# A hybrid convolution and MLP block on one core: diagonals made by GpSimd selects, larger buffer rings and another hand-written order

## The chip, the core and the metric

The kernel runs on one core of a Trainium2 chip. A core has a matrix engine (TensorE, in the profile PE, with its weight loads PEld), a vector engine (VectorE, DVE), an activation engine (ScalarE, ACT), a general engine (GpSimd, POOL) and a sequencer for transfers (SyncE, SP; SPq is its queue). The engines run side by side and wait for one another through semaphores. Operands lie in an on-chip memory of 128 partitions, matmuls write to eight PSUM banks of 128 x 512 f32, and transfers run on 16 DMA engines. The metric is the device time of one execution in microseconds (us), lower is better.

## What is computed

S = 2048 rows, D = 512 channels, F = 1792; inputs and output are bf16.

```python
def _A_ref(q, k, v, shift_k, ssm_k, ssm_D):      # ks = 4
    for t in range(ks):
        k_shift = k_shift + k_pad[:, t:t + S, :] * shift_k[:, ks - 1 - t][None, None, :]
    kv = k_shift * v
    y = irfft(rfft(pad(kv)) * rfft(pad(ssm_k)))[:S]
    y = y + kv * ssm_D
    return q * y
def _B_ref(x, w1, w2, w3, w4):
    h = gelu(layernorm(x) @ w1)
    hs = concat(four quarters of h, shifted by +1, -1, +2, -2 rows) @ w2
    x1 = x + hs
    return x1 + gelu(layernorm(x1) @ w3) @ w4
h = A_q + _A_ref(layernorm(A_q), A_k, A_v, A_shift_k, A_ssm_k, A_ssm_D)
return h + _B_ref(layernorm(h), B_w1, B_w2, B_w3, B_w4)
```

So a four-tap filter over the rows of k, a gate by v, a long convolution over the rows with one filter for each channel, a gate by q, and then a block of two small matmuls with row shifts and an MLP from 512 to 1792 to 512 channels.

## The kernel before, in words

The rows are cut into two halves, s = 0 and 1, of eight blocks of 128 rows. The long convolution is done by matmuls: a two-step transform of the filter (signals F0 and F1) and of the gated k (A0 and A1), products of the spectra, and a two-step inverse. Everything is cut into 812 named tasks. `plan.add` (from L268 on) lists them with their engines and dependencies, and the string `ORDER` (L31 on) fixes by hand which task comes next, on which engine (S for SP, P for PE, V for DVE, A for ACT, G for POOL, M for a double-width eviction on ACT) and in which buffers. Each engine runs its own tasks in the order of that string, and waits at a task until its inputs are there; nothing behind it on that engine passes it. The DMA queue is SP's: the loads, the transfers between the transform's steps and the stores all go through it in order.

In what follows a task is called by its name and indices:

- Lk, Lf, Lv, Lq: loads of k (transposed, with the taps in the last columns of each row), the convolution filter, v and q; the first index is the half.
- skf.c (L298): copies the four taps of channel block c, bf16, from the loaded k to f32 scalars `sskf`. dg.c (L300 to L312): from them four 128 x 128 diagonal matrices in `diag`, each the identity times one tap, by four instructions on DVE (L309) or ACT (L307).
- K.gc (L444): the four-tap filter as seven matmuls against the diagonals, for half a half (g = 0 to 3) and channel block c. KV.gc (L452): the gate by v, on DVE, out of PSUM.
- S1 (L391), E1, X (L407), S2 (L415), E2: first transform step, its eviction out of PSUM (L259, on ACT or DVE), the transfer that turns the partitions, the second step, and its eviction. For F1 the second eviction adds F0's spectrum (L427, DVE).
- P (L476): products of the spectra, 128 x 1024, all on DVE, into a ring `prs` of four buffers. I2 (L486): the inverse's first step, EV its eviction into a ring `vst` of two, XI (L497) its transfer, I1 (L504) its second step. There are 16 products for s = 0 and 32 for s = 1.
- bits, cons, ftv, fta, ft, ttv, tta, tts, f2v, f2a, f2s, tt, f2: building the transform's tables in several steps that go to and fro between DVE, POOL and ACT. `cons` (L331 to L335, POOL) needs `bits` (L324 to L328, DVE); ft is the table that S2 needs.
- dr (L296): adds ssm_D to the filter's first row. Q, QV, QP, QN: statistics of q. Y (L616): normalised q, into a ring `z_t` of two. H (L619): the gate, with the residual. HS, uw, rr, hn, hb: the layer norm of H.
- LT, TE (L673, L259): transposes by PE and their evictions; for some pairs of blocks they are two writes to memory and a transposing load on SP instead (L666, L668). xT holds the transposed blocks, a ring of three. W (L702) and U (L706): the first matmul and its gelu. X2 (L725), S, SS, R: the second matmul with the row shifts, and its sums. ux, r1, xn, lb, LX, EX: the second layer norm and transposes. M (L780), G (L784), O (L793), Z (L795), OUT: the MLP's two matmuls, the gelu, the last sum and the store.

Each half has its W, X2, M and O tasks. The MLP of s = 0 runs among the products of s = 1.

Of the kernel before, what the change touches and what calls it, by code (L numbers as in the profile page):

```python
# [17 lines left out]
KW = NB * 129 + 4  # L18
# [13 lines left out]
002S 004S 003S 005S 031V 041V 042G 043G 000S 029P0 030P 059P23 001S 007S 061P45 006S 062V 067P67 010S 033V 037V 032V 069P01 008S 070V 009S 060A 068A  # L32
034V 063P23 064A 065P45 066A 023S 049G 022S 038A 035V 091P60 039V 055P23 099P71 100V 036A 044V 056A 057P45 058A 040V 101P0 102V 103P1 104V 050V 045A
355V 051A 046G 047V 105P7 106V 048A 093P2 095P3 076S 119P45 120A 094V 115P01 354V 077S 054G 024S 075S 015S 096V 097P7 078S 116A 074S 073S 092V 098V
020S 071S 358V 121P23 122A 117P45 107P01 357V 053G 108A 118V 072S 111P67 113P23 021S 114V 016S 127S 109P01 112A 110A 123S 088P4567 089V 128S 090A
085P0123 087A 082P4567 083A 356V 086V 231P21 084A 079P4501 232V 124S 080V 081A 129S 125S 131P6723 130S 134P0145 132V 133A 136A 126S 144V0 143V1 352V
147V2 146V3 135A 014S 137P2367 019S 233P4 011S 139A 018S 145P01670 154V0 153V1 138A 148P 157V2 149A 156V3 223P50 224V 150A 155P01231 158P 159M 160A
187P67 353V 344S 229P5 234V 163V0 164V1 017S 151S 152S 230V 012S 351V 188A 140P0123 141A 235P4 142A 166V2 167V3 161S 162S 165P67010 168P 173V0 013S
359G 169A 174V1 227P5 170A 171S 172S 176V2 175P23671 177V3 178P 180A 199P01 228V 237P5 179V 236V 200A 181S 182S 238V 225P6 226V 343S 360G 361G 052A
362V0 191P23 193P01 192A 189P45 190A 194V 204S 203S 195P67 196A 201P23 202V 197P01 198A 183P45 239P67 365G1 366V 371G1 367A 207S 241P23 208S 184P01  # L40
363V 368G0 364A 242V 243P45 245P23 240A 369V 386G 372V 244A 246A 210S 373A 374V0 209S 206S 205S 257S 387G 185P67 247P01 377V1 375V 380G0 248A 378V
214P2345 215V 370A 249P67 250A 379A 388G 399V 186P01 381V 027S 255S 389G0 392G1 251P23 252A 253P67 254A 376A 383G1 390P00 393P2 259S 216V 211P4567
394V 391A 395P3 258S 384V 212V 382A 220P0145 400G 401G 402A2 405A3 403P21 404A 346S 213V 412G 413G 221V 406P6 397P7 347V 396A 263P0123 385A 398A 407V
# [802 lines left out]
```

## Time and profile before

| what | us |
|---|---|
| three runs: median, lowest, highest | 217.25, 216.3, 217.52 |
| the profiled execution, its device time | 216.0 |
| its span (first to last instruction in the trace) | 214.2 |
| PE busy in it | 198.7 |
| DVE, ACT, POOL busy | 147.9, 128.3, 72.3 |

The span is what the trace shows; 1.8 us of the device time lie outside it. A row of the list of groups gives the line, the engine, the operation, what it writes and reads, the count, then the busy time, the mean of one in ns, and the idle time of the engine just before with what ended it. A row of the timeline gives the start, the duration, the engine, the line and, in brackets, the idle time before it. A row of the table by stretches gives the length of the stretch and the busy time of each engine in it.

### The profile page before, as it was taken

Reading aid. Unit: us, or ns where it says so; the run is one execution under the profiler, and the core shown is the slowest. Engines: PE = TensorE matmul, PEld = TensorE weight load, DVE = VectorE, ACT = ScalarE, POOL = GpSimd, SP = SyncE. Lnnn points to the kernel's source line nnn. Section 1 sums busy time; section 2 is a strip of 40 time slices with the busy share of each in tenths; the row PEclk is TensorE's granted clock in tenths of the full one; section 3 lists DMA queues with packets and bytes.
Section 4 is the critical chain, followed back from the end, with each engine's and each line's share of the span. In section 5 each row is a group of like instructions: output and inputs, shape, how many; then the busy total and the mean of one; then the engine's idle time right before and its main releaser. Section 6 shows DMA issues by size and latency. Waiting matters only on the chain.

```text
span 214.2 us, 5136 instructions
## 1 busy us (share of the span) xinstructions
PE 198.7 (93%) x1980; PEld 114.8 (54%) x1980; DVE 147.9 (69%) x331; ACT 128.3 (60%) x210; POOL 72.3 (34%) x194
## 2 busy tenths in 40 slices
PE   7699858898979999999999999799999999999993
PEld 5254324342246646644655774466788887444441
DVE  7999998998999999889894985318687000005621
ACT  4678987889999676961960896345445757000000
POOL 7943000593786436400005883304615000000000
PEclk9999999999999999999999999999999999999998
DMA  6999699978679965030553015850644400000212
GB/s 197 343 386 340 251 362 329 231 203 296 244 252 300 408 249 150 0 100 1 77 148 101 2 23 113 163 122 13 160 99 104 117 2 0 3 0 24 97 50 73
DMA packets 30809, 32.85 MB, mean 153 GB/s; under 512 B 20545, under 2 KB 22594, under 8 KB 30530
## 3 DMA queue, kind: packets, MB, share of 16 engines
q1 hardware_dynamic: 30786, 32.54, 50.0%
q8 instruction: 15, 0.25, 0.5%
q14 instruction: 8, 0.07, 0.1%
HBM read 13.13 MB, written 4.46 MB: 82 GB/s over the span
## 4 chain that ended last, share of the span: by engine, by line
PE 73%; ACT 9%; DMA 7%; issue 4%; DVE 3%; SPq 3%; DVEq 0%; ACTq 0%
PE ps L780 23%; PE ps L793 21%; PE ps L725 6%; PE ps L702 6%; PE ps L486 6%; ACT r_a L259 3%; PE ps L444 3%; DMA r_dg<-dhb 2%; PE ps L504 2%; DMA r_fx<-in_fx_dram 2%; PE ps L415 2%; ACT r_z L259 2%; PE ps L391 2%; ACT junk L603 2%; DMA r_z<-r_vs 2%
## 5 line engine op out<-in xcount | busy, mean ns | idle before, releaser
L780 PEld LDWEIGHTS <-r_k 128*128 128x128 bf16 x448 | 43.2, 98 | 9.4 <-issue 3.2
L795 DVE TENSOR_TENSOR r_v<-ps,r_v 128x512 bf16<-128x512 f32 x16 | 10.7, 687 | 39.4 <-issue 31.4
L780 PE MATMUL ps<-r_dg,r_k 128*128 128x256 bf16 x280 | 32.9, 273 | 0.0
L476 DVE TENSOR_TENSOR r_p<-r_a,r_f 128x1024 bf16<-128x1024 bf16 x48 | 30.7, 685 | 2.5 <-PE ps L486 1.9
L259 ACT CAST r_a<-ps 128x1024 bf16<-128x1024 f32 x25 | 24.2, 1021 | 1.2 <-PE ps L391 0.6
L780 PE MATMUL ps<-xtx,r_k 128*128 128x256 bf16 x168 | 20.2, 273 | 0.0
L728 DVE SCALAR_TENSOR_TENSOR r_q<-r_v,hrr,ps 128x512 bf16<-128x512 bf16 x16 | 11.8, 741 | 9.0 <-PE ps L725 8.9
L444 PE MATMUL ps<-r_dg,r_k 128*128 128x256 bf16 (+3 forms) x112 | 16.0, 288 | 2.1 <-ACT r_f L259 1.7
L486 PE MATMUL ps<-r_p,ttab 32*64 32x512 bf16 x384 | 15.6, 383 | 1.2 <-DVE r_p L476 0.5
L259 ACT CAST r_vs<-ps 128x1024 bf16<-128x1024 f32 (+1 forms) x14 | 14.5, 1075 | 3.2 <-PE ps L486 2.3
L444 PEld LDWEIGHTS <-r_k 128*128 128x128 bf16 x112 | 9.3, 98 | 11.0 <-issue 5.6
L702 PEld LDWEIGHTS <-r_fx 128*128 128x128 bf16 x128 | 12.2, 98 | 5.4 <-issue 1.5
L751 POOL TENSOR_TENSOR xrr<-xrr,mhalf 128x2 f32<-128x2 f32 x8 | 7.0, 876 | 20.4 <-DVE xrr L748 20.0
L784 ACT ACTIVATE r_v<-ps 128x512 bf16<-128x512 f32 x14 | 8.0, 596 | 9.7 <-PE ps L780 9.6
L702 PE MATMUL ps<-r_dg,r_fx 128*128 128x256 bf16 x96 | 11.8, 273 | 1.7 <-DMA r_dg<-dhb 1.2
L603 ACT ACTIVATE junk<-r_v 128x512 bf16<-128x512 bf16 x14 | 9.0, 642 | 6.8 <-DVE r_v L619 5.9
L793 PE MATMUL ps<-w4s,r_kv 128*128 128x512 bf16 x56 | 12.7, 379 | 0.0
L619 DVE SCALAR_TENSOR_TENSOR r_v<-ps,qsd,z_t 128x512 bf16<-128x512 f32 x16 | 11.4, 746 | 1.9 <-PE ps L504 1.6
L793 PE MATMUL ps<-w4s,r_v 128*128 128x512 bf16 x56 | 12.6, 379 | 0.0
L793 PE MATMUL ps<-w4s,r_a 128*128 128x512 bf16 x56 | 12.2, 379 | 0.0
L793 PE MATMUL ps<-w4s,r_f 128*128 128x512 bf16 x56 | 12.2, 379 | 0.0
L391 PEld LDWEIGHTS <-f 128*32 128x32 bf16 x256 | 5.6, 96 | 11.7 <-issue 7.0
(182 smaller groups left out, 353.9 us busy)
## 6 DMA issues: line engine op xcount, KB each, us to landing
r_z<-r_vs SPq DMA_DIRECT2D x16, 256.0 KB, 3.5
r_k<-in_kt_dram SPq DMA_DIRECT2D x8, 259.0 KB, 5.0
r_v<-in_v_dram SPq DMA_DIRECT2D x4, 512.0 KB, 6.3
r_q<-in_q_dram SPq DMA_DIRECT2D x8, 256.0 KB, 6.3
r_f<-r_f SPq DMA_DIRECT2D x8, 256.0 KB, 4.9
r_a<-r_a SPq DMA_DIRECT2D x8, 256.0 KB, 3.0
r_f<-r_a SPq DMA_DIRECT2D x8, 256.0 KB, 3.1
r_a<-r_z SPq DMA_DIRECT2D x8, 256.0 KB, 6.2
```

What stands on the lines that cost most here:

```text
L259: (act.copy if e in "AM" else on[e].tensor_copy)(o, i)
L444: nc.tensor.matmul(o[:, (d + j0) * P:(d + j1 + 1) * P], lhsT=kT[s][c][:, bb, x:x + P], rhs=diag[:, c, j0:j1 + 1, :].rearrange("p j x -> p ...
L476: on[e].tensor_tensor(out=prs[:, sl[0], :, :], in0=sp[a][:, kl, t, :, :], in1=gv, op=MUL)
L486: nc.tensor.matmul(ps[64 * t:64 * t + 64, bk[h], :], lhsT=ttab[32 * h:32 * h + 32, 2 * kl + t, 2 if x else xx, :], rhs=prs[32 * h:32 * h + ...
L603: act.activation(junk[:], x, ACT.Square, accum_out=sq[:, i, 1:2])
L619: vec.scalar_tensor_tensor(out=h_sb[s][:, b, :], in0=ps[:, got(("I1", s, b // 2))[b % 2], :], scalar=qsd[:, i:i + 1], in1=z_t[:, got(("Y", ...
L702: nc.tensor.matmul(ps[:, sl[0], j * 256:(j + 1) * 256], lhsT=w1s[:, k, m * P:(m + 1) * P], rhs=xt[:, k, :], start=(k == 0), stop=(k == DC ...
L725: nc.tensor.matmul(ps[:, sl[0], :], lhsT=h1T[s][:, m, bb, x:x + P], rhs=w2s[:, m, :], start=(m == 0), stop=(m == DC - 1))
L728: vec.scalar_tensor_tensor(out=q_sb[:, s, b, :], in0=h_sb[s][:, b, :], scalar=hrr[:, 4 * s + b // 2, 0, b % 2:b % 2 + 1], in1=ps[:, got((" ...
L780: nc.tensor.matmul(ps[:, sl[0], j * 256:(j + 1) * 256], lhsT=w3s[:, k, fc * P:(fc + 1) * P], rhs=xt[:, k, :], start=(k == 0), stop=(k == D ...
L793: nc.tensor.matmul(ps[:, sl[0], :], lhsT=gb[:, fc, (b % 2) * P:(b % 2 + 1) * P], rhs=w4s[:, fc, :], start=(fc == 0), stop=(fc == FC - 1))
L795: add(("Z", s, b), {V: 0.61}, lambda e, sl, b=b: vec.tensor_tensor(out=h_sb[s][:, b, :], in0=ps[:, got(("O", s, b))[0], :], in1=h_sb[s][:, ...
```

## The change

Four edits go together.

1. The taps come as pairs of bf16, zero and tap, which read as one f32. So skf and `sskf` are gone, and each row of k has eight columns of taps instead of four. dg.c on POOL is now one affine select that writes all four diagonals of a channel block; on DVE and ACT it is four instructions as before.
2. Rings: `prs` 8 instead of 4, `vst` 3 instead of 2, `z_t` 4 instead of 2 (Y may run four blocks ahead of H instead of two), xT 4 instead of 3. A scratch area for transfers is set to 1024.
3. In the head of the program, POOL writes the small tables for `bits` ahead of its index patterns instead of behind them.
4. A new `ORDER`, of 808 tasks. The numbers of tasks behind skf shift by four.

```diff
-KW = NB * 129 + 4
+KW = NB * 129 + 8
...
-002S 004S 003S 005S 031V 041V 042G 043G 000S 029P0 030P 059P23 001S 007S 061P45 006S 062V 067P67 010S 033V 037V 032V 069P01 008S 070V 009S 060A 068A
...
+005S 029P0 008S 004S 007S 009S 003S 033V 010S 030P 031V 037V 002S 095P10 006S 036G 000S 024S 063P23 343G 038G 021S 065P45 035A 001S 087P01 020S 039G
...
-    r_p = raw("r_p", 4 * 2 * D)
-    r_vs = raw("r_vs", 2 * 4 * D)
+    r_p = raw("r_p", 8 * 2 * D)
+    r_vs = raw("r_vs", 3 * 4 * D)
...
-    z_t = ct("z_t", 2, D, dt=F32)
+    z_t = ct("z_t", 4, D, dt=F32)
...
+    xty = ct("xty", DC, 256)
...
-    sskf = ct("sskf", DC * 4, dt=F32)
...
-    plan = Plan({"ps": 8, "pr": 4, "vs": 2, "z": 2, "nb": 4, "xt": 3, "kv": 2, **{"gb%d" % i: 1 for i in range(6)}})
+    plan = Plan({"ps": 8, "pr": 8, "vs": 3, "z": 4, "nb": 4, "xt": 4, "kv": 2, **{"gb%d" % i: 1 for i in range(6)}})
...
-    for c in range(DC):
-        add(("skf", c), {V: 0.17, GP: 0.22, A: 0.22}, lambda e, sl, c=c: copy(e, sskf[:, 4 * c:4 * c + 4], kw[:, 0, c, NB * 129:KW]), [("Lk", 0, c)])
...
+            if e == GP:
+                tap = r_k[:, c * KW + NB * 129:(c + 1) * KW].rearrange("p (j x) -> p j x", x=2)[:, :, 1:2]
+                pool.affine_select(out=diag[:, c], in_=tap.to_broadcast([P, 4, P]), compare_op=OP.is_equal, fill=0.0, base=0,
+                                   pattern=[[0, 4], [-1, P]], channel_multiplier=1)
+                return
...
-        add(("Y", s, b), {GP: 0.76, A: 0.79, V: 0.47}, qn, [("QN", s)] + ([("H", s, b - 2)] if b > 1 else [("H", 0, b + 6)] if s else []), take=[("z", 1)], port="VG")
+        add(("Y", s, b), {GP: 0.76, A: 0.79, V: 0.47}, qn, [("QN", s)] + ([("H", s, b - 4)] if b > 3 else [("H", 0, b + 4)] if s else []), take=[("z", 1)], port="VG")
...
-    nc = _bacc.Bacc("TRN2", target_bir_lowering=False, num_devices=1)
+    nc = _bacc.Bacc("TRN2", target_bir_lowering=False, num_devices=1, dynamic_dma_scratch_size=1024)
...
-    taps = _np.broadcast_to(a["A_shift_k"].reshape(DC, P, 4), (2, DC, P, 4))
-    kt = _np.concatenate([kt, taps.astype(kt.dtype)], axis=3)
+    taps = _np.zeros((2, DC, P, 4, 2), kt.dtype)
+    taps[..., 1] = a["A_shift_k"].reshape(DC, P, 4)
+    kt = _np.concatenate([kt, taps.reshape(2, DC, P, 8)], axis=3)
```

The two orders with their tasks by name, the first part of each queue:

```
before
SP    Lf.01 Lf.03 Lf.02 Lk.00 Lsd Lf.00 Lk.02 Lk.01 Lv.01 Lk.03 Lv.00 Lq.02 Lq.01 X.F011 X.F012 Lq.03 X.F010 Lk.10 X.F013 ...
PE    warm S1.F010 F011 F030 F031 F020 F021 K.00 S1.F000 K.10 S1.F001 K.11 K.12 K.13 K.01 K.02 S1.A030 A020 K.03 S1.A031 ...
DVE   bits E1.F011 skf.0 dg.0 dr E1.F031 skf.1 skf.2 dg.2 KV.10 fta dg.3 KV.11 KV.12 f2a Q.04 tta KV.13 KV.01 Q.03 KV.02 ...
ACT   E1.F010 F030 F020 F021 dg.1 skf.3 E1.F000 F001 ft f2s tts E1.A030 A020 A031 A000 A010 A001 E2.F031 ...
POOL  cons ftv f2v ttv f2 tt QV.0 QP.0 QN.0 Y.01 Y.03 Y.02 ...
after
SP    Lk.00 Lk.03 Lf.03 Lk.02 Lv.00 Lf.02 Lv.01 Lf.01 Lk.01 Lsd Lq.03 Lq.00 Lf.00 Lv.11 Lq.02 Lv.10 Lk.11 Lk.10 Lq.01 X.F011 X.F001 ...
PE    warm K.10 S1.F030 F031 K.00 K.03 K.13 K.02 K.12 S1.F010 F011 F020 K.11 K.01 S1.F000 F001 F021 S1.A000 A010 ...
DVE   dg.0 bits ttv tta KV.03 KV.00 KV.10 KV.13 KV.02 KV.12 Q.06 Q.00 dr KV.11 KV.01 E1.F001 A000 A020 f2a fta Q.03 E1.A001 ...
ACT   dg.2 E1.F030 tts E1.F031 F010 F011 F020 F000 F021 A010 A011 A030 A031 f2s ft E1.A021 E2.F010 F011 F001 F000 F021 A001 F031 F030 A010 A011 A020 ...
POOL  dg.3 edge0 cons ftv tt dg.1 f2v f2 QV.0 QP.0 QN.0 Y.02 Y.01 Y.00 ...
```

In the middle, before has the four I1.0 tasks between the S1.A1 tasks, after has the four I1.0 in a row and then the S1.A1. In the second half, before runs W.10, O.05, X2.07, X2.06, O.04, W.11, W.12, W.13 behind the last I1.1 task; after runs the seven M.02, O.04, W.10, O.05, X2.06, X2.07, W.11, W.12, W.13 behind it. Here W.12 stands for the two W tasks of that pair of blocks, and so for the others.

More of the change, by code (lines that the diff above doesn't have):

```diff
@@ L146, in body @@
     wv = view(r_z, 0, G, "p (k h d) -> p k h d", k=NB, h=2)
-    prs = r_p[:].rearrange("p (i r d) -> p i r d", i=4, r=2)
-    vst = r_vs[:].rearrange("p (i h d) -> p i h d", i=2, h=4)
+    prs = r_p[:].rearrange("p (i r d) -> p i r d", i=8, r=2)
+    vst = r_vs[:].rearrange("p (i h d) -> p i h d", i=3, h=4)
     h1T = [view(r, 0, DC * NB * HX, "p (c b x) -> p c b x", c=DC, b=NB) for r in (r_h, r_f0)]
@@ L164, in body @@
     xtx = ct("xtx", DC, 256)
-    xT = [view(r_dg, 0, DC * 256, "p (c x) -> p c x", c=DC), view(r_dg, DC * 256, DC * 256, "p (c x) -> p c x", c=DC), xtx]
+    xty = ct("xty", DC, 256)
+    xT = [view(r_dg, 0, DC * 256, "p (c x) -> p c x", c=DC), view(r_dg, DC * 256, DC * 256, "p (c x) -> p c x", c=DC), xtx, xty]
     ident = ct("ident", P)
@@ L311, in body @@
     for c in range(DC):
-        add(("dg", c), {V: 0.8, A: 1.19, GP: 1.45}, dg(c), [("skf", c)], port="VG")
+        add(("dg", c), {V: 0.8, A: 1.19, GP: 0.85}, dg(c), [("Lk", 0, c)], port="VG")
     sv = small("sv", 8, F32)
```

82 lines of the change are left out of this document (40 added, 42 removed).

## The prediction

> **What bounds the kernel now.** I read the page's head and its slices first, to see which engine is full when.
>
> ```profile
> span 214.2 us, 5136 instructions
> PE   7699858898979999999999999799999999999993
> DVE  7999998998999999889894985318687000005621
> ACT  4678987889999676961960896345445757000000
> GB/s 197 343 386 340 251 362 329 231 203 296 244 252 300 408 249 150 0 100 1 77 148 101 2 23 113 163 122 13 160 99 104 117 2 0 3 0 24 97 50 73
> ```
>
> PE is full from slice 12 to the end but for a dent at slice 25 and the tail. In the first twelve slices (62 us) DVE is the fullest. So I cut the span at the points that the order gives: 49.7 is the first I1.0, 62.5 the first W.
>
> ```profile
> core 0: us, PE busy (x) PEld busy (x) DVE busy (x) ACT busy (x) POOL busy (x), PEclk, DMA share, GB/s
> 0.00:5.00 5.00, 3.73 (x40) 2.65 (x44) 3.67 (x22) 2.25 (x4) 3.72 (x44) 1.00 0.62 199
> 5.00:15.00 10.00, 8.00 (x84) 3.87 (x77) 9.45 (x24) 7.78 (x12) 7.29 (x18) 1.00 1.00 356
> 15.00:49.70 34.70, 29.60 (x462) 12.88 (x459) 33.10 (x50) 30.10 (x33) 10.36 (x17) 1.00 0.92 289
> 49.70:62.50 12.80, 10.75 (x124) 3.83 (x121) 12.38 (x30) 12.43 (x23) 9.18 (x22) 1.00 0.66 244
> 62.50:130.00 67.50, 67.39 (x754) 40.31 (x754) 59.24 (x142) 47.11 (x86) 29.04 (x65) 1.00 0.44 136
> 130.00:145.00 15.00, 13.74 (x88) 8.19 (x86) 5.44 (x15) 6.85 (x13) 3.12 (x10) 1.00 0.67 133
> 145.00:210.00 65.00, 65.00 (x441) 43.04 (x440) 23.93 (x55) 21.81 (x44) 9.55 (x20) 1.00 0.23 59
> 210.00:214.20 4.20, 0.48 (x3) 0.00 (x0) 0.69 (x1) 0.00 (x0) 0.00 (x0) 0.80 0.09 31
> ```
>
> PE's idle time is 10.4 us before 62.5 (1.27 + 2.00 + 5.10 + 2.05), 0.1 up to 130, 1.3 from 130 to 145, none to 210, and 3.7 in the tail. No matmul is added or removed, so the span can fall only by idle time of PE. The tail is the last Z and its store, in either order. Before 62.5, DVE idles 3.9 us and ACT 9.9, of which 1.3 and 2.8 lie in the first 5 us: these two set the pace there. Three places carry the rest of the argument:
>
> ```profile
> 33.16 2.50 DVE L476 TENSOR_TENSOR r_p<-r_a,r_f 128x1024 bf16<-128x1024 bf16 x4 [0.66 <-issue]
> 49.71 1.04 PE L504 MATMUL ps<-r_z,f 128*128 128x512 bf16 x4
> 62.50 1.03 PE L702 MATMUL ps<-r_dg,r_fx 128*128 128x256 bf16 x8 [0.48 <-ACT r_dg L259]
> 138.90 3.67 PE L702 MATMUL ps<-r_dg,r_fx 128*128 128x256 bf16 x32 [1.21 <-DMA r_dg<-dhb]
> ```
>
> In the first, the fifth product has no free buffer of `prs` until I2.000 has read one. In the last, W.12 waits for a transposing load.
>
> **The change part by part.**
>
> *Diagonals and taps.* The unit prices, and what stands nearest to the affine select and to ttv on DVE:
>
> ```profile
> L309 DVE TENSOR_SCALAR r_dg<-ident,sskf 128x128 bf16<-128x128 bf16 x12 | 2.7, 291 | 0.1
> L259 DVE CAST sskf<-r_k 128x4 f32<-128x4 bf16 x3 | 0.9, 328 | 0.1
> masks.py:199 POOL TENSOR_SCALAR_AFFINE_SELECT ident<-ident 128x128 bf16<-128x128 bf16 x1 | 0.3, 292 | 0.1
> L658 POOL TENSOR_SCALAR r_k<-r_v,hrr,hnm 128x512 bf16<-128x512 bf16 x6 | 4.7, 794 | 0.3 <-DVE hnm L644 0.3
> L357 POOL TENSOR_TENSOR r_a<-r_a,r_p 128x512 int32<-128x512 int32 x1 | 1.3, 1277 | 0.1
> L359 DVE TENSOR_SCALAR r_a<-r_a 128x512 int32<-128x512 int32 x1 | 0.4, 404 | 0.0
> L516 POOL TENSOR_TENSOR qnm<-qst 128x8 f32<-128x8 f32 x1 | 3.6, 3580 | 21.5 <-DVE qst L508 21.5
> L452 DVE TENSOR_TENSOR r_kv<-ps,r_v 128x512 bf16<-128x512 f32 x16 | 10.5, 681 | 0.6 <-issue 0.3 <-ACT r_f L259 0.3
> L616 DVE TENSOR_SCALAR z_t<-r_q,qrs,qnm 128x512 f32<-128x512 bf16 x5 | 3.1, 630 | 0.1
> L614 ACT ACTIVATE z_t<-r_q,qnm,qrs 128x512 f32<-128x512 bf16 x2 | 1.5, 806 | 0.0
> L259 ACT CAST r_a<-ps 128x1024 bf16<-128x1024 f32 x25 | 24.2, 1021 | 1.2 <-PE ps L391 0.6 <-PE ps L415 0.4 <-DVE r_a L259 0.2
> ```
>
> DVE loses three skf (0.9 us) and two of its three dg (8 x 0.23 = 1.8, from 2.7 for 12). One Y up to the first I1.0 goes to other engines (0.6). It takes over ttv, two operations on 128 x 512 int32 that it doesn't show; its 128x512 operation at 681 ns gives 1.4. Both ends: 0.8 (two like the 404 ns of its 512-wide int32 AND) and 2.6 (two like POOL's 1277). That makes -1.9 for DVE. ACT keeps one dg, loses one skf (0.2) and gains a Y (0.8): +0.6. The evictions only change places, eight on each side for DVE. Since either engine can evict, I take half the balance: **-0.6** at the first I1.0; ends -1.9 (DVE alone counts) and +0.6 (ACT alone counts).
>
> The select writes 512 columns. Its bounds are 0.29 (one fixed price) and 1.17 (four of the 128-wide); I take 0.8, as POOL's 512-wide operation has. POOL is free for dg.3 at 4.5 (below), so dg.3 is over near 5.7 if its load comes a little later, and dg.1, behind tt, near 12.2, when K.11 that needs it is still behind other matmuls (below). So the selects themselves cost nothing; without that cover, POOL's 0.8 each.
>
> [...]
>
> *The new wait.* ttv now stands right behind bits on DVE and needs cons from POOL.
>
> ```profile
> 2.84 0.68 DVE L231 TENSOR_SCALAR f<-r_p,mk 128x64 bf16<-128x64 bf16 x4
> 4.38 0.10 POOL L250 MEMSET r_p<- 128x1 f32 x1
> 4.87 0.22 DVE L327 TENSOR_REDUCE sv<-r_p 128x8 f32<-128x64 f32 x1
> 5.13 0.23 DVE L328 TENSOR_SCALAR mk<-l,sv 128x4 bf16<-128x4 int32 x1
> 5.86 0.28 POOL L333 TENSOR_SCALAR kf<-k,sv 128x8 f32<-128x8 int32 x1
> ```
>
> From `sv` (5.09) to the end of `kf` (6.14) it is 1.05 us, and DVE's own work covers 0.27 of it. In the new order dg.0 runs ahead of bits, from 3.5 to about 4.7 (four at 291 ns), and cons would start near 6.3, behind dg.3. So DVE stands for 0.8 us with eight KV, two Q and the first evictions behind it. Lower end 0.3 (PE is late with the first K and DVE would have waited for those anyway), upper end 2.0, if dg.3 and edge0, ahead of cons on POOL, hold it. **+0.8.**
>
> *k first.* Nineteen loads, 5.8 MB, now stand ahead of X.F on SP, where thirteen stood. At the page's rates (197, 343, 386, 340 GB/s in slices of 5.36 us) that is moved by about 18.4 us. PE's side, from these rows:
>
> ```profile
> 1.64 4.25 DMA r_fx<-in_fx_dram
> 9.62 0.61 PE L391 MATMUL ps<-r_fx,f 128*32 128x512 bf16 x8
> 10.16 1.04 PE L444 MATMUL ps<-r_dg,r_k 128*128 128x512 bf16 x7
> 17.88 1.86 DVE L452 TENSOR_TENSOR r_kv<-ps,r_v 128x512 bf16<-128x512 f32 x3
> 13.46 1.16 ACT L346 ACTIVATE ftab<-r_a,negpi 128x1024 bf16<-128x1024 int32 x1
> 31.62 0.40 PE L486 MATMUL ps<-r_p,ttab 32*64 32x512 bf16 x2
> ```
>
> dg.0 ends near 4.7; the third load is there at 5.9 as before. Then K.10, two S1, five K, three S1, K.11 and K.01 at about 1.0 and 0.55 run without a gap to about 15.6, and the last KV ends near 16.3, where before it ended at 19.7. The filter pays: its last S1 and E1 come after that (near 18), so X.F starts at 18. That is when the loads are through, so the queue costs nothing more. ft needs fta, which on DVE is now behind three evictions and f2a: about 22.4, then f2s and ft to 23.9. From there ACT has E1.A021 and nine or ten E2 at about 1.0 before E2.A011 frees I2.000's banks: 34.4, where before it ran at 31.62. Those 2.8 us I put at **0**, because with eight buffers of `prs` DVE makes products and Q ahead while it waits, and has less to do between I2.000 and I1.0: eleven products, five KV and five evictions, where twelve, seven and three, two Q and a Y stood, 1.6 us less with evictions at 1.2, KV and Q at 0.68 and products at 0.63. The other end is +2.8.
>
> *Rings.* Eight product buffers take away the wait at 33.16: **-0.7** (ends -0.7 and 0, if it comes back in front of ACT). The other rings hide behind PE or ACT: 0.
>
> *The middle.* Four I1.0 in a row take all eight banks, and S1.A1 waits for H to free them. ACT then has six HS, seven E1 and two TE up to the first W, as before plus one TE (about 0.5), against two LT more that PE has behind it by then (0.4). **+0.1**; ends -0.5 and +1.5 (DVE's H, uw, hn and two E2.F1 come ahead of hb.02, which that W needs).
>
> *Second half.* Between the last I1.1 and W.12 stood W.10, O.05, two X2, O.04 and W.11, some 11 us; now seven M (6.1 us) stand there too. A transposing load that came 1.21 us late has its cover: **-1.2** (end 0: a new one). In exchange only six W and seven X2 (11.3 us) are between X2.07 and M.030. What must happen in them (S, SS, ux, r1, xn, lb, two writes and the transposing load) sums to about 10 us, so it holds by 1.
>
> Sum: -0.6 + 0.8 + 0 - 0.7 + 0.1 - 1.2 = **-1.6**. On the profiled span of 214.2 that is 212.6, and 214.4 for its execution of 216.0. The median of the runs shown is 217.25, 1.25 above the profiled one; the predicted time is put there: **215.7**.
>
> **The rivals.**
>
> *A, the first stage shortens in earnest.* DVE alone counts up to I1.0 (-1.9), its wait costs 0.3, the ring gives 0.7, the middle -0.5: -2.8, with W.12's 1.2 it is -4.0, so 213.2. For it: DVE has 4.1 us idle before 62.5, ACT 9.9. Against: ACT's load grows.
>
> *B, a transfer takes the place of the one relieved.* M.030 or another W waits 1.2 us: -0.4, so 216.9. For it: the cover holds by 1 us only. Against: SP's queue is empty there.
>
> *C, the filter is too late.* The 2.8 us by which I2.000 slips are not made up, because EV, XI and I1.0 follow one another, and the wait for cons costs its 0.8; with the rest, +2.8 - 1.6 = +1.2, so 218.5, and up to 220 with the middle's upper end. It decides from the point where I2.000 runs later than about 33.5 us while DVE stands idle between 24 and 40. For it: ACT's row of ten evictions from 23.9. Against: DVE, the fuller one, has less to do.
>
> *D, the select is slow.* If it takes as long as POOL's slowest row, 3.6 us, dg.3 and edge0 end at 8.6 and hold cons, and DVE, for 2.3 us: +0.7, so 218.0. For it: that row, on eight columns only. Against: the 292 ns of the one select in the trace. [...] That the edits of taps and rings do nothing by themselves is in A to C.
>
> **How the numbers follow.** Forecast 0.38, A 0.20, B 0.13, C 0.25, D 0.04. About 0.5% (1.1 us) is what can be told from no change. The forecast (own range 214.3 to 216.6) is faster by more in four of five cases; A always is; B is no change; C and D are slower. Faster 0.51, same 0.19, slower 0.30. The range takes in A and most of C: 212.6 to 219.2.
>
> **What would show it.** Right: no dg on DVE but one of 4 instructions; selects of 0.7 to 1.2 us; DVE idle 0.8 us ahead of ttv; PE without a gap from 6 to 15; I2.000 near 34; the first I1.0 between 48.5 and 50; the first W near 62; no wait of W for a transposing load. Wrong: I1.0 past 51 (C), or before 47.5 (A), or PE idle by over 0.5 us between 65 and 205 (B).

## The result, and the profile after

| what | us |
|---|---|
| before, four runs beside the changed kernel: median, lowest, highest | 216.97, 216.3, 217.52 |
| after, four runs: median, lowest, highest | 213.97, 213.66, 214.16 |
| ratio after to before, with its 95% interval | 0.9861 (0.9829 to 0.9894) |
| a second comparison, among the experiments: median, ratio | 214.40, 0.9915 (0.9885 to 0.9945) |
| span of the profiled execution, before and after | 214.2, 212.4 |
| first I1.0, first W, first I1.1, before | 49.71, 62.50, 116.25 |
| the same, after | 51.18, 64.86, 115.71 |
| end of the last matmul, before and after | 210.48, 208.62 |

The kernel became faster by 0.9 to 1.4%, 1.8 us between the two profiled executions, 3.0 us between the first medians and 1.9 between the second (216.32 and 214.40). The page's head and two of its slices, of the kernel after:

```profile
span 212.4 us, 5087 instructions
PE 196.5 (93%) x1962; PEld 118.2 (56%) x1980; DVE 145.6 (69%) x327; ACT 126.4 (59%) x206; POOL 73.7 (35%) x179
PE   5999957988779999999999999999999999999992
PEclk9999997999999999999999999999999999999999
```

PE's first slice fell from 7 to 5, and slices 6 to 12 have holes as before. (The one 7 in the row of the clock is a dip of the granted clock to 0.50 for some 3.4 us from 34.5 us on, behind 3 us in which PE was busy for only half of the time. Other executions of these orders have such dips too (in the one with the longer warm-up, below, the granted clock between 25 and 35 us has a mean of 0.67). In the second profiled execution of this kernel it lasts 10.2 us, from 29.3 on, and the first I1.0 still comes at 51.13 us, where it comes at 51.18 here, so the dip is not what makes the first stage late.) The table by stretches, of the kernel after, shows where:

```profile
core 0: us, PE busy (x) PEld busy (x) DVE busy (x) ACT busy (x) POOL busy (x), PEclk, DMA share, GB/s
0.00:5.00 5.00, 2.57 (x21) 2.26 (x22) 3.37 (x24) 1.83 (x3) 4.17 (x45) 1.00 0.58 184
5.00:15.00 10.00, 9.95 (x81) 5.08 (x80) 6.76 (x14) 4.32 (x8) 6.85 (x15) 1.00 1.02 366
15.00:51.18 36.18, 30.67 (x484) 13.83 (x480) 34.72 (x49) 33.81 (x38) 12.00 (x16) 0.95 0.80 264
130.00:145.00 15.00, 14.79 (x95) 9.16 (x95) 6.26 (x20) 6.46 (x14) 1.83 (x3) 1.00 0.66 131
```

Between 130 and 145 us PE has 14.79 busy where it had 13.74, so the wait of W.12 for its transposing load is gone, as forecast. Between 5 and 15 us DVE has only 6.76 busy where it had 9.45, although PE is full there. The timeline of the kernel after tells why, and gives the prices that the prediction had to bound:

```profile
4.61 0.63 POOL L300 TENSOR_SCALAR_AFFINE_SELECT r_dg<-r_k 128x512 bf16<-128x512 bf16 x1
4.75 1.87 PE L443 MATMUL ps<-r_dg,r_k 128*128 128x512 bf16 x7 [1.39 <-DVE pb L323]
6.93 0.69 DVE L351 TENSOR_TENSOR r_a<-r_p,kf 128x512 int32<-128x512 int32 x1 [0.82 <-POOL kf L332]
11.39 3.68 DVE L451 TENSOR_TENSOR r_kv<-ps,r_v 128x512 bf16<-128x512 f32 x6 [2.17 <-PE ps L443]
33.95 0.40 PE L485 MATMUL ps<-r_p,ttab 32*64 32x512 bf16 x2 [0.30 <-ACT r_a L258]
51.18 3.61 PE L503 MATMUL ps<-r_z,f 128*128 128x512 bf16 x15 [0.50 <-ACT r_a L258]
64.86 1.04 PE L701 MATMUL ps<-r_dg,r_fx 128*128 128x256 bf16 x8
115.71 3.62 PE L503 MATMUL ps<-r_z,f 128*128 128x512 bf16 x16
```

A select takes 0.63 us (taken: 0.8) and DVE stands 0.82 us for `kf` (taken: 0.8). PE stands 1.39 us between its warm-up and K.10, and K.10 then takes 1.87 us; before it took 1.04. It is not K.10 alone. The same shape of matmul, in groups of one microsecond each, from 9 to 10 and from 12 to 13 us:

```profile
L443 PE MATMUL ps<-r_dg,r_k 128*128 128x384 bf16 x2 | 1.0, 524 | 0.0
...
L443 PE MATMUL ps<-r_dg,r_k 128*128 128x384 bf16 x3 | 1.0, 326 | 0.0
```

Up to about 10.5 us every matmul is this slow (524 ns against 326), while the column of the granted clock shows 1.00. That 1.00 is no measurement: the first record of the clock in this trace stands at 10.59 us, just where the matmuls become fast, and the column counts a time without a record as full clock. DVE waits 2.17 us for the first K, and the first stage ends 1.47 us later than before, where the forecast had it earlier. The first W is 2.36 us late. Then the new order makes up 2.90 us up to the first I1.1 (115.71 against 116.25), where nothing was expected. That is the puzzle for the experiments.

One count from the two orders is needed for it. PE's tasks come in four tile shapes, as the rows print them: S1 128 x 32, S2 64 x 32, I2 32 x 64, all others 128 x 128. Going down PE's queue, the shape changes 73 times in the order of before (27 up to the first I1.0, 46 from there to the first I1.1, then never) and 47 times in that of after (21, 26, none).

### The profile page after: what moved, and what is told of

The parts are those of the page before. It is cut to its first block, busy times and chain, and to the rows that moved or that the text cites. A ratio compares the mean times of both kernels' runs of the same rounds, so it can differ in the third digit from the quotient of the medians.

```text
span 212.4 us, 5087 instructions
## 1 busy us (share of the span) xinstructions
PE 196.5 (93%) x1962; PEld 118.2 (56%) x1980; DVE 145.6 (69%) x327; ACT 126.4 (59%) x206; POOL 73.7 (35%) x179
## 4 chain that ended last, share of the span: by engine, by line
PE 69%; ACT 6%; issue 2%; DVE 0%; ACTq 0%; DVEq 0%
PE ps L779 23%; PE ps L792 23%; PE ps L701 7%; PE ps L724 6%; PE ps L485 4%; ACT r_z L258 2%; ACT r_a L258 2%; PE ps L503 2%; PE ps L414 2%; PE ps L672 1%; ACT junk L602 1%; PE ps L390 1%; ACT L368 1%; PE ps L443 0%; DVE r_v L794 0%
## 5 line engine op out<-in xcount | busy, mean ns | idle before, releaser
L779 PEld LDWEIGHTS <-r_k 128*128 128x128 bf16 x448 | 43.6, 98 | 7.6 <-issue 1.2
L779 PE MATMUL ps<-r_dg,r_k 128*128 128x256 bf16 x224 | 25.8, 273 | 0.0
L783 ACT ACTIVATE r_f<-ps 128x512 bf16<-128x512 f32 x14 | 7.6, 603 | 23.6 <-PE ps L779 23.5
L258 ACT CAST r_vs<-ps 128x1024 bf16<-128x1024 f32 x14 | 13.5, 1018 | 9.6 <-PE ps L485 8.7
L443 PEld LDWEIGHTS <-r_k 128*128 128x128 bf16 x112 | 10.0, 104 | 10.7 <-issue 6.1
L258 ACT CAST r_f<-ps 128x1024 bf16<-128x1024 f32 x14 | 13.4, 1042 | 4.1 <-PE ps L390 4.1
L615 POOL TENSOR_SCALAR z_t<-r_q,qrs,qnm 128x512 f32<-128x512 bf16 x13 | 11.7, 915 | 9.9 <-DVE r_v L618 9.7
L750 POOL TENSOR_TENSOR xrr<-xrr,mhalf 128x2 f32<-128x2 f32 x8 | 5.9, 738 | 21.9 <-DVE xrr L747 21.5
L779 PE MATMUL ps<-xty,r_k 128*128 128x256 bf16 x112 | 12.7, 272 | 0.0
L779 PE MATMUL ps<-xtx,r_k 128*128 128x256 bf16 x112 | 12.7, 273 | 0.0
L451 DVE TENSOR_TENSOR r_kv<-ps,r_v 128x512 bf16<-128x512 f32 x16 | 10.4, 683 | 2.7 <-PE ps L443 2.6
```

The lines of the kernel that those rows point to most:

```text
L258: (act.copy if e in "AM" else on[e].tensor_copy)(o, i)
L443: nc.tensor.matmul(o[:, (d + j0) * P:(d + j1 + 1) * P], lhsT=kT[s][c][:, bb, x:x + P], rhs=diag[:, c, j0:j1 + 1, :].rearrange("p j x -> p ...
L451: vec.tensor_tensor(out=kvs[:, got(("K", g, 0), "kv")[0], :, c * P:(c + 1) * P], in0=ps[:, got(("K", g, c))[0], :].rearrange("p (b x) -> p ...
L615: on[e].tensor_scalar(out=z_t[:, sl[0], :], in0=qs, scalar1=qrs[:, i:i + 1], scalar2=qnm[:, i:i + 1], op0=MUL, op1=ADD)
L779: nc.tensor.matmul(ps[:, sl[0], j * 256:(j + 1) * 256], lhsT=w3s[:, k, fc * P:(fc + 1) * P], rhs=xt[:, k, :], start=(k == 0), stop=(k == D ...
```

## The experiments

All times are medians beside runs of the kernel before on the same chip; the ratio is to those. In the first four experiments the kernel before had 216.40 us, in the next four 216.32, then 216.57 and 216.28.

**The old order on the new buffers, POOL's tables and taps.**

```diff
-ORDER of after
+ORDER of before without skf
```

> The changed kernel with the task order of the kernel before (only skf left out); taps in place, larger rings and POOL's earlier small tables stay, and no affine select is used, since that order puts all dg on DVE and ACT. Theory (the gain is the order's): 0.0 to 0.7 us under before, for the 1.1 us of skf that go, and the order's 73 changes of matmul form on PE stay. Rival (taps and rings give the gain): 2 to 3 us under before, as the changed kernel.

Measured: 216.18 us, ratio 0.9988 (0.9950 to 1.0026). The gain is the order's; rings and taps by themselves bring nothing that can be told. (The selects are not in this run: the old order makes its diagonals on DVE and ACT.) Two rows of its timeline show why the ring is worth nothing in the old order:

```profile
33.61 2.50 DVE L478 TENSOR_TENSOR r_p<-r_a,r_f 128x1024 bf16<-128x1024 bf16 x4 [1.32 <-ACT r_a L261]
...
139.62 3.67 PE L704 MATMUL ps<-r_dg,r_fx 128*128 128x256 bf16 x32 [1.47 <-DMA r_dg<-dhb]
```

The fifth product no longer waits for a buffer, but it waits 1.32 us for ACT's eviction of its operand instead.

**The new order up to the first I1.1, the old one behind it.**

```diff
-PE  I1.10 I1.11 I1.12 I1.13 M.020 M.022 M.021 M.024 M.026 M.023 M.025 O.04 W.101 W.100 O.05 X2.06 X2.07 W.111 ...
+PE  I1.10 M.020 I1.11 M.023 I1.12 M.025 M.024 M.021 M.026 M.022 I1.13 W.100 W.101 O.05 X2.07 X2.06 O.04 W.110 ...
```

> The changed kernel's order up to the first I1.1 task, then the remaining tasks in the order of before. Theory (the new second half only takes away the wait of W.12): PE waits again about 1.2 us for a transposing load, and the time is 1.0 to 1.5 us over the changed kernel's. Rival (that wait was hidden anyway, or the gain lies ahead of I1.1): within 0.4 us of the changed kernel.

Measured: 215.49 us, ratio 0.9948 (0.9914 to 0.9983). The changed kernel has 0.9861 and 0.9915 in its two comparisons, so by the ratios the new second half is worth 0.7 to 1.9 us behind the new first half. The forecast's 1.2 lies in that, but the interval of the second comparison (0.9885 to 0.9945) overlaps with this one. From the first I1.1 to the end of the last matmul the profile has 93.76 us, against 92.91 in the changed kernel and 94.23 in the kernel before. The wait that the theory named did not come back: W.12 waits 0.30 us only, so where the rest of the difference lies was not found.

**The old order up to W.000, the new one behind it.**

```diff
-order of after up to W.000
+order of before up to W.000
```

> The order of before up to its first W task, then the remaining tasks in the changed kernel's order. Theory (the new head is a loss: its first W starts 2.4 us later with only some 0.5 us more of PE's work behind it, and it is made up by fewer changes of matmul form, 47 in place of 73 over the whole order, at about 0.1 us each): first W near 62.3, 58 changes of form, and 0.5 to 1.5 us under the changed kernel. Rival (the new head does DVE and ACT work ahead that pays later): equal to the changed kernel or over it by up to 1.5 us.

Measured: 216.39 us, ratio 0.9985 (0.9948 to 1.0022). The theory fell. Its timeline at the seam:

```profile
64.35 0.60 PE L675 MATMUL ps<-ident,nbx 128*128 128x128 bf16 x4 [1.79 <-DVE nbx L660]
...
66.12 1.87 PE L704 MATMUL ps<-r_dg,r_fx 128*128 128x256 bf16 x8 [0.73 <-ACT r_dg L261]
```

PE waits 1.79 us for DVE and 0.73 for ACT, and the W behind that runs at half speed (1.87 us for eight matmuls that take 1.04). The granted clock was 0.50 there, from 63.8 to 70.6 us. So it seems that the new middle lives on what DVE and ACT have ready at that point, and that a late first W in the new order is partly work done ahead; a cut there tells nothing of either half.

**A longer warm-up, so that PE does not stand before K.10.**

```diff
-        for i in range(20):
+        for i in range(36):
```

> The changed kernel with 36 warm-up matmuls in place of 20, so that PE runs on until dg.0 is there at 4.7 us. In the changed kernel PE stands from 3.35 to 4.75 and its matmuls then take about 1.6 times as long until 10.5 us. Theory (the standing costs PE its speed, and the late K hold DVE, 2.2 us idle ahead of KV): matmuls of K at 326 ns for 384 columns from the start, DVE's idle time ahead of the first KV under 0.8 us, and 0.7 to 1.8 us under the changed kernel. Rival (the stage is set by the loads, DVE or ACT later on): KV starts earlier but the time stays within 0.4 us.

Measured: 214.13 us, ratio 0.9871 (0.9811 to 0.9931), the changed kernel's within the interval. Four rows of its timeline, K.10, the first I1.0, O.01 behind the last I2, and the first I1.1:

```profile
4.75 1.03 PE L446 MATMUL ps<-r_dg,r_k 128*128 128x512 bf16 x7
...
49.91 3.61 PE L506 MATMUL ps<-r_z,f 128*128 128x512 bf16 x16 [0.51 <-ACT r_a L261]
...
108.39 6.22 PE L795 MATMUL ps<-w4s,r_v 128*128 128x512 bf16 x28
...
115.17 2.10 PE L506 MATMUL ps<-r_z,f 128*128 128x512 bf16 x9 [0.57 <-issue]
```

K.10 is back at 1.03 us and the first I1.0 comes 1.27 us earlier, so in this execution the slow matmuls account for 1.3 us of the first stage. Another run below, again with 36 warm-up matmuls and K.10 at 1.03 us, has its first I1.0 at 49.14. The lead is still there at O.01, which follows the last I2 at 108.39 us (109.61 in the changed kernel's second profiled execution, whose row is shown below). Then I1.10 waits 0.57 us behind two O. The row names no releaser ("issue"); its inputs come by the transfers XI, issued behind the last evictions, which the two O must cover. What is left at the last matmul is 0.3 us, too little to tell. So the theory was right on the first stage, and for the time the rival holds.

**Changes of shape put back.**

```diff
-PE  I2.100 I2.101 I2.102 I2.103 X2.01 X2.00 X2.04
+PE  I2.100 X2.01 I2.101 X2.00 I2.102 X2.04 I2.103
...
-PE  I2.120 I2.121 I2.122 I2.123 M.000 M.004 M.001 M.002 M.005 M.006 M.003 I2.130 I2.131 I2.132 I2.133
+PE  I2.120 M.000 I2.121 M.004 I2.122 I2.123 M.001 M.002 M.005 I2.130 M.006 I2.131 M.003 I2.132 I2.133
```

> The changed kernel, in whose TensorE order some tasks of the middle change places among themselves: X2.01, X2.00 and X2.04 go between I2.100 to I2.103, and the seven M.00 are mixed with I2.120 to I2.133. Nothing is added, and the other engines' orders stay. A 32-row matmul task now stands beside a 128-row one 14 times more often. Theory: from the first I1.0 to the first I1.1 the changed kernel saved 3.2 us of busy TensorE by 20 fewer such changes, so a change costs about 0.16 us; the time rises by 1.4 to 2.3 us, the ratio to the kernel before by 0.007 to 0.011 over the changed kernel's in the same call, and I2 in the middle takes near 0.6 us each where it took 0.53. Rival: the busy time fell for another reason (fewer waits inside a task), the changes of shape are free, and the time stays within 0.5 us.

Measured: 219.62 us, ratio 1.0158 (1.0127 to 1.0188), 5.2 us above the changed kernel's 214.40 beside the same runs. Its timeline, a new wait, I2 and X2 in turn, and three more of its waits:

```profile
77.44 1.02 PE L727 MATMUL ps<-r_fx,r_h 128*128 128x512 bf16 x4 [0.66 <-DVE r_f L429]
78.39 0.64 PE L488 MATMUL ps<-r_p,ttab 32*64 32x512 bf16 x16
78.97 1.04 PE L727 MATMUL ps<-r_fx,r_h 128*128 128x512 bf16 x4
79.93 0.64 PE L488 MATMUL ps<-r_p,ttab 32*64 32x512 bf16 x16
...
83.24 0.38 PE L675 MATMUL ps<-ident,r_k 128*128 128x128 bf16 x4 [0.80 <-ACT r_vs L261]
...
85.74 3.65 PE L782 MATMUL ps<-r_dg,r_k 128*128 128x256 bf16 x32 [0.69 <-ACT r_dg L261]
...
107.03 2.78 PE L782 MATMUL ps<-r_dg,r_k 128*128 128x256 bf16 x24 [1.14 <-ACT r_vs L261]
```

And the same kinds of task in a row, in the changed kernel's second profiled execution:

```profile
78.45 2.77 PE L724 MATMUL ps<-r_fx,r_h 128*128 128x512 bf16 x12
81.05 0.39 PE L672 MATMUL ps<-ident,nbx 128*128 128x128 bf16 x4
...
107.75 1.93 PE L485 MATMUL ps<-r_p,ttab 32*64 32x512 bf16 x64
109.61 6.22 PE L792 MATMUL ps<-w4s,r_v 128*128 128x512 bf16 x28
```

Read starts, not durations, since matmuls in a row overlap: O's in the changed kernel last 379 ns each and start 216 ns apart. In turn, an I2 and an X2 take 79.93 - 78.39 = 1.54 us; in a row, (81.05 - 78.45) / 3 = 0.87 for an X2 and (109.61 - 107.75) / 4 = 0.47 for an I2, 1.34 together. So two changes cost 0.20 us, and 14 more of them 1.4. Most of the rest of the 5.2 us is waits: the last of four I2 now comes later, so its eviction does too, and what is behind that on ACT and DVE (0.66 + 0.80 + 0.69 + 1.14 = 3.3 us in the rows above). Over the whole stretch from the first I1.0 to the first I1.1 the trace says the same: PE is busy for 63.59 us where the changed kernel's second execution has 61.47, and idle for 6.48 where that has 3.07. So 2.1 us are busy time, 0.7 more than the 14 changes account for. The price is real; the theory's bound of 2.3 us missed the waits.

The traces show the price one by one as well. In the second execution of the changed kernel the last matmul of an M is followed 0.11 us later by the first of an O, just as by the next one inside an M, and 0.20 us later by the first of an I2. Of its 37 changes of shape at full clock and without a wait, 35 cost 0.09 us like this one, while 31 of 32 steps between different tasks of the same shape cost nothing. So it is the shape that costs, not the change of task.

**The new second half behind the old order.**

```diff
-order of after up to I1.10
+order of before up to I1.10, without skf
```

> The order of before (without skf) up to the first I1.1 task, and from there the order of after; all else as in the changed kernel. Theory: the second half is worth 1.3 us by itself (1.21 of it the wait of W.12 for a transposing load) and does not need the new head, so the time is 1.3 us under that of the kernel with the whole old order, ratio to before near 0.993, and W.12 waits for no transfer. Rival: as with the old head up to the first W, the new part lives on work that the new order had done ahead, new waits appear, and the ratio stays at 0.998 or more.

Measured: 216.18 us, ratio 0.9984 (0.9953 to 1.0016). No gain over the whole old order (216.18 too). In the one execution that was profiled W.12 no longer waits, and from the first I1.1 to the end of the last matmul it takes 93.63 us where the old order took 94.90. The runs of both kernels spread over some 3 us (214.7 to 217.2 and 214.7 to 217.7), the changed kernel's over about 1.3. By its medians the rival holds; by its profile the theory does. That is left open.

**The diagonals back on DVE.**

```diff
-DVE   dg.0 bits ttv tta KV.03 KV.00 KV.10 KV.13 KV.02 KV.12 ...
-POOL  dg.3 edge0 cons ftv tt dg.1 f2v ...
+DVE   dg.0 bits dg.3 ttv tta KV.03 KV.00 KV.10 KV.13 KV.02 dg.1 KV.12 ...
+POOL  edge0 cons ftv tt f2v ...
```

> The changed kernel with dg.3 and dg.1 on DVE again, by four instructions each, dg.3 behind bits and dg.1 behind KV.02; POOL makes no diagonals. Theory: in the changed kernel DVE stands for 3.0 us between 6 and 12 us (0.82 for kf, 2.17 for the first K), so the 1.8 us of diagonals that the selects took off DVE weigh little: the first I1.0 comes at most 0.6 us later and the ratio stays within 0.003 of the changed kernel's in this call. Rival (DVE's load counts, as the forecast's balance had it): the first I1.0 is 0.6 to 1.9 us later, and the ratio rises by 0.003 to 0.009.

Measured: 214.29 us, ratio 0.9912 (0.9880 to 0.9945); the changed kernel beside the same runs 0.9915. Its first I1.0:

```profile
50.57 3.61 PE L506 MATMUL ps<-r_z,f 128*128 128x512 bf16 x16 [0.51 <-ACT r_a L261]
```

In this one execution it comes 0.6 us earlier, not later. But PE's slow start was shorter in it as well: its matmuls become fast at 7.8 us, where those of the changed kernel do at 10.6 in the first profiled execution and at 8.8 in the second. So the row cannot price the diagonals; the medians can. The selects save DVE 1.8 us in a stretch in which it stands for 3.0, and are worth nothing that can be told here.

**The changed kernel once more.**

> The changed kernel unaltered, beside the other three on the same chip: its ratio to before should lie at 0.983 to 0.989 as in the first comparison, and it gives the others their mark. If the first comparison was luck of the chip, it lies above 0.99.

Measured: 214.40 us, ratio 0.9915 (0.9885 to 0.9945). That misses the range that was expected and lies above the 0.99 from which on the first comparison was to be put down to its chip; the two intervals overlap (0.9885 to 0.9894) and no more. So the gain is some 0.9 to 1.4%, and the first figure may have been a lucky one. In this execution the trace has all 1980 matmuls (18 are missing in the first one), so PE's busy time from the first I1.0 to the first I1.1 is taken from it. One row for the kernel before and one for this:

```profile
49.71:116.25 66.54, 64.38 (x773) 34.14 (x769) 60.67 (x129) 48.23 (x82) 27.82 (x60) 1.00 0.55 180
```

```profile
51.13:115.67 64.54, 61.47 (x769) 35.76 (x769) 59.78 (x127) 47.35 (x77) 28.36 (x64) 1.00 0.59 193
```

The same tasks take PE 2.9 us less busy time (61.47 for 64.38), while it stands idle 0.9 us more (3.07 for 2.16).

**The price by itself.** A kernel of matmuls alone:

```diff
+    for n in range(16):
+        I2()
+    for n in range(16):
+        M(4 + n % 4)
+    for n in range(16):
+        I2()
+        M(4 + n % 4)
...
+    for g in (1, 2, 4, 8):
+        gate(g)
+        for n in range(12):
+            M(4 + n % 4)
```

> A kernel of matmuls alone on zeros, with the shapes of this one; nothing of the reference is computed and the output is zeros. Sixteen I2-shaped groups (32 x 64, 16 matmuls) in a row, sixteen M-shaped groups (128 x 128, eight matmuls) in a row, then the two alternating, then four and four; the same with X2-shaped groups, and M with S1-shaped groups (128 x 32). Theory: each change between small-tile and full matmuls costs 0.09 to 0.15 us, so an I2 and an M that take 0.47 to 0.51 and 0.87 us in a row take 1.55 to 1.65 together when they alternate, and near 1.40 with four and four. Rival (no price by itself, the kernel's groups were slowed by their waits): 1.34 to 1.38 in every order. It opens with 20 warm-up matmuls of 128 x 128 and a stop of TensorE for about 1 to 1.5 us: if that stop is what left the changed kernel's first matmuls at half speed, the M-shaped groups behind it take about 1.7 us instead of 0.87 for some 5 us; later stops of about 1, 2, 4 and 8 us behind long work show how long a stop it takes.

Its timeline: sixteen I2 in a row, sixteen M in a row, the beginning of the two in turn, and of four and four; then sixteen X2 in a row, the first I2 in turn with X2, and seventeen S1, from the last of which on S1 and M take turns:

```profile
26.39 7.11 PE L64 MATMUL ps<-xb,wb 32*64 32x512 bf16 x256
33.44 14.15 PE L54 MATMUL ps<-xa,wa 128*128 128x256 bf16 x128
47.52 0.64 PE L64 MATMUL ps<-xb,wb 32*64 32x512 bf16 x16
...
72.26 1.93 PE L64 MATMUL ps<-xb,wb 32*64 32x512 bf16 x64
...
77.72 1.93 PE L64 MATMUL ps<-xb,wb 32*64 32x512 bf16 x64
...
94.23 13.76 PE L58 MATMUL ps<-xb,wa 128*128 128x512 bf16 x62
107.92 0.64 PE L64 MATMUL ps<-xb,wb 32*64 32x512 bf16 x16
...
132.51 7.52 PE L69 MATMUL ps<-xb,wb 128*32 128x512 bf16 x136
139.97 1.05 PE L54 MATMUL ps<-xa,wa 128*128 128x256 bf16 x8
140.94 0.61 PE L69 MATMUL ps<-xb,wb 128*32 128x512 bf16 x8
...
142.47 0.62 PE L69 MATMUL ps<-xb,wb 128*32 128x512 bf16 x8
```

An I2 in a row takes (33.44 - 26.39) / 16 = 0.44 us and an M (47.52 - 33.44) / 16 = 0.88. In turn a pair takes (72.26 - 47.52) / 16 = 1.55, 0.23 more than 1.32, so 0.11 for each change. With four and four it is (77.72 - 72.26) / 4 = 1.37 for a pair, 0.18 more for eight tasks with two changes, 0.09 each. An X2 in a row takes (107.92 - 94.23) / 16 = 0.86, a pair of I2 and X2 in turn (132.51 - 107.92) / 16 = 1.54: 0.12 for each change (two of the 64 matmuls in the row of X2 are missing in the trace, so the 0.86 may be 0.01 more). An S1 takes (139.97 - 132.51) / 17 = 0.44, and S1 and M in turn 142.47 - 140.94 = 1.53: 0.11. No engine but PE works there, so the price is PE's own. All of the 101 changes there that can be read one by one take 0.09 us more from start to start. The same kernel's stops of PE, each with the matmuls behind it:

```profile
4.07 22.39 PE L54 MATMUL ps<-xa,wa 128*128 128x256 bf16 x192 [0.58 <-DVE xa L74]
...
183.47 10.64 PE L54 MATMUL ps<-xa,wa 128*128 128x256 bf16 x96 [1.38 <-DVE xa L74]
197.07 12.31 PE L54 MATMUL ps<-xa,wa 128*128 128x256 bf16 x96 [2.96 <-DVE xa L74]
```

Behind long work a stop of 1.38 us costs nothing (96 matmuls in 10.64 us, 0.88 for eight) and one of 2.96 costs 1.67 us (a later one of 6.14 costs 1.36). At the start, 2.3 us of warm-up and a stop of only 0.58 leave the next matmuls slow: 24 groups take 22.39 us where 24 x 0.88 = 21.1. The stop at the start was meant to last 1 to 1.5 us and came out at 0.58, so the changed kernel's own stop was not rebuilt. The kernel before has one of that length, in front of K.00, when PE had been fast since 4.4 us (S1's groups of four matmuls start 0.21 us apart from there on, 0.39 and 0.37 before):

```profile
8.65 1.03 PE L444 MATMUL ps<-r_dg,r_k 128*128 128x512 bf16 x7 [1.50 <-ACT r_f L259]
```

K.00 takes 1.03 us behind it. So the likely reading is that the stop of 1.39 us in the changed kernel hurts because PE had not reached full speed before it: its warm-up matmuls, of 128 columns, start 107 ns apart, where later ones of 128 columns (in K and in the transposes) have the next 56 ns behind them.

**The long warm-up with the diagonals on DVE.**

```diff
-        for i in range(20):
+        for i in range(36):
...
-POOL  dg.3 edge0 cons ftv tt dg.1 f2v ...
+POOL  edge0 cons ftv tt f2v ...
```

> The changed kernel with 36 warm-up matmuls for 20, and with dg.3 and dg.1 on DVE. Each alone brought the first I1.0 forward (by 1.3 and 0.6 us) without a measurable gain at the end. Theory: DVE is full from 62 to 110 us (47.5 of 48 us busy in the changed kernel), so what the head gains reaches the end in part only: the first I1.0 near 49.5, ratio to before 0.985 to 0.991. Rival: the gains add up to the end, 0.982 or less.

Measured: 214.48 us, ratio 0.9875 (0.9834 to 0.9916). The ratio is where the theory had it, but the first I1.0 came at 51.11 us and not at 49.5. That execution does not tell whether the two gains add: K.10 again took 1.91 us, although PE did not stand before it, and the first KV waited 0.93 us for the load of v, which landed at 10.15 us (at 8.30 with the long warm-up alone). So 36 warm-up matmuls made K.10 fast in two of the three executions that were profiled with them.

**The long warm-up and more cover for XI.**

```diff
-PE   O.00 I1.10 I1.11 I1.12 I1.13 M.020 M.022 M.021 ...
+PE   O.00 M.020 M.022 I1.10 I1.11 I1.12 I1.13 M.021 ...
-ACT  G.006 HS.10 HS.12 HS.11 HS.13 HS.14 G.021 G.020 ...
+ACT  G.006 G.020 G.022 HS.10 HS.12 HS.11 HS.13 HS.14 G.021 ...
```

> The changed kernel with 36 warm-up matmuls for 20, and M.020 and M.022 with their gelus ahead of I1.10 instead of behind I1.13. With the long warm-up alone the four last I2 ended at 108.39 us where the changed kernel had them end at 109.6, but I1.10 then waited 0.57 us for the transfer XI. Theory: the gain of the head is there up to that point and is lost at this wait; two M (1.75 us) cover it, the first I1.1 comes behind them without a wait, and the time falls by 0.5 us or more against the long warm-up alone: ratio 0.984 or less, span under 212. Rival: the M only move the wait (banks of PSUM, H on DVE), and the ratio stays at 0.987 or more.

Measured: 214.77 us, ratio 0.9913 (0.9876 to 0.9949). The rival. Its timeline, O.01 behind the last I2, and M.024 behind I1.1 and M.021:

```profile
107.62 6.22 PE L795 MATMUL ps<-w4s,r_v 128*128 128x512 bf16 x27
...
121.28 2.78 PE L782 MATMUL ps<-xtx,r_k 128*128 128x256 bf16 x24 [0.70 <-DVE r_v L621]
```

At 107.62 us it is 2.0 us ahead of the changed kernel, and I1.10 follows without that wait. But the two M are then missing behind I1.13, where they had stood between I1.1 and the work that needs H's banks: PE waits 0.70 us for H there, 0.25 in I1.1, and the last matmul ends at 208.41 us, 0.2 ahead.

**The old first stage, the new order from the first I1.0 on.** At that point both orders have sent the same matmuls.

```diff
-order of after up to I1.00
+order of before up to I1.00, without skf
```

> The order of before (without skf) up to the first I1.0, and from there the order of after; all else as in the changed kernel. At that point both orders have sent the same matmuls to TensorE, and DVE, ACT and POOL stand alike but for three Y and edge0. Theory: the new first stage costs (first I1.0 at 51.2 us where the old one has it at 49.7 to 50.5), and the gain is made behind I1.0, with 26 changes of shape up to the first I1.1 where the old order has 46; so with the old first stage the first I1.0 comes near 50.2, the first I1.1 near 115, and the time is 0.5 to 1 us under the changed kernel's: ratio 0.982 to 0.989. Rival: the new first stage is what feeds the stages behind it (as with the cut at the first W, where new waits of 2.5 us came up), and the ratio is 0.995 or more.

Measured: 213.63 us, ratio 0.9874 (0.9838 to 0.9911). The rival falls, and the gain lies behind the first I1.0:

```profile
49.71 3.62 PE L506 MATMUL ps<-r_z,f 128*128 128x512 bf16 x16
...
114.69 3.62 PE L506 MATMUL ps<-r_z,f 128*128 128x512 bf16 x16
```

The first I1.0 is at 49.71 us, as in the kernel before, the first I1.1 at 114.69, 1.0 us ahead of the changed kernel, and the span is 211.4. Its median is the lowest of all kernels here, but not told apart from the changed kernel's (0.9861 and 0.9915).

## Why the prediction was right in its sum and wrong in its steps

| stretch | forecast | profiled executions |
|---|---|---|
| up to the first I1.0 | -0.6 + 0.8 + 0 - 0.7 = -0.5 | +1.47 |
| from there to the first I1.1 | +0.1 | -2.01 |
| from there to the last matmul | -1.2 | -1.32 |
| behind it | 0 | +0.06 |
| sum | -1.6 | -1.8 |

The predicted 215.7 us lies 1.7 above the median of 213.97, and the sign, the range and the sum held; of the forecast's own, narrower range (214.3 to 216.6) the first median lies just outside, the second, 214.40, inside. But two stretches were wrong by 2 us each, with opposite signs; that the sum came out was luck.

- **The step that failed** is the sentence "No matmul is added or removed, so the span can fall only by idle time of PE." From the first I1.0 to the first I1.1, PE's idle time rose by 0.9 us and its busy time fell by 2.9 with the same matmuls. The shape of the tiles changes 20 times less there. At the 0.09 to 0.12 us that the kernel of matmuls alone gave, that is 1.8 to 2.4 us. The 0.5 to 1.1 that remain were not separated. The old first stage with the new order behind it leaves the finding as it is: the stretch took 64.98 us there, where the kernel before takes 66.54. What in PE makes a change cost that was not shown.
- **The same order buys more than the price.** Putting 14 changes back cost 5.2 us, of which 1.4 are the changes and 3.3 waits, for ACT above all. This fits with four I2 in a row ending early, so that their evictions and transfers have cover; that was not tested apart. The old ring of four cannot hold the eight products that such a row reads. So it is likely that the ring pays here and not where the forecast put it, but no run took the ring away in the new order.
- **Ring, -0.7: wrong** in the old order. There the wait came back 1.32 us long in front of ACT, the end that the prediction gave as 0.
- **Balance of DVE and ACT, -0.6: wrong.** The diagonals on DVE again changed the ratio by nothing. DVE had 3.0 us of standing in that stretch, which the balance did not ask for. Whether they would cost something once PE starts fast was not shown. (Rival A gives DVE 4.1 us of idle time before 62.5; by the prediction's own table it is 3.9.)
- **The wait for cons, 0.8: its size was right (0.82) and its cost was none** in this execution, since DVE stood another 2.17 us behind it for K.10 and K.03.
- **k first, 0: wrong.** I2.000 ran at 33.95 us, forecast 34.4, and the first I1.0 at 51.18, past the 51 that was named for rival C. But C also had DVE idle between 24 and 40 us, and it was busy for 15.48 of these 16. Some 1.3 of the 1.47 us come from PE's slow start, as the longer warm-up shows, not from the late filter that C named. K.10 was taken at its price in the old order, where it ran at 10.16 us and PE had been fast since 4.4. In the kernel of matmuls alone 1.38 us of standing did no harm behind long work, and 2.96 cost 1.67 us; what makes PE start slowly, and what ends it, was not shown. That the lost 1.3 us are not had back at the end was shown by the same run and the one with more cover: it is lost at the first I1.1 (to XI, most likely) and, with cover there, at H.
- **The middle, +0.1: wrong before the first W and behind it.** Up to the first W the stretch became 0.89 us longer, and from there to the first I1.1, where nothing was forecast, 2.90 shorter.
- **Second half, -1.2: right in size** behind the new first half, by two ways (the profile's -1.32, and 0.7 to 1.9 us when its order is put back). In the kernel before, the wait of W.12 is 1.21 of it; with the old second half behind the new first half it was only 0.30. M.030's transposing load was not late, so rival B did not come. Behind the old order no gain of the median was found, which stays open.
- **Selects: 0.63 us**, a little under the 0.7 to 1.2 that were named as a sign, and hidden as forecast; rival D is out.

## What to carry to other kernels

Count the changes of tile shape in TensorE's order before saying that a full TensorE cannot get faster: reordering the same matmuls was worth some 2 us here, at about 0.1 us for each change. When a sum comes out right, check its stretches at points where both kernels have done the same work; cut a hybrid at such a point too: the cut at the first W starved its second part here. And what was freed on an engine in a stretch in which it stood for another was worth nothing here, so look for the wait behind the one that is added or taken away.

## What the runs showed of the hardware that was not expected

- A change between 128 x 128 tiles and 32 x 64 or 128 x 32 ones costs TensorE 0.09 to 0.12 us, with no other engine at work; a change of task within one shape costs nothing (31 of 32 steps).
- An affine select of 128 x 512 bf16 takes 0.63 us on GpSimd, where the 128 x 128 one took 0.29: less than in proportion.
- Matmuls ran at half speed between 4.75 and 10.5 us in the changed kernel (from the start of one of K's of 384 columns to the next start 320 ns, later 162), where the column of the granted clock shows 1.00, because the trace has no record of the clock before 10.59 us; there the durations alone show the slow start. Behind the stop of 2.96 us in the kernel of matmuls alone, the column fell to 0.50 (from 198 to 200 us).
- The end of the slow start moves from execution to execution: 10.6 and 8.8 us in two of the same kernel, and with 36 warm-up matmuls and no stop 4.4, 4.8 and, with the diagonals on DVE, 6.7.
